# Attention and a GELU block on one core: k of the first batch through SyncE's hardware queue as fp32, masks of the first batch on VectorE, loads and squares in another order

## The chip, the core and the metric

The kernel runs on one core of a Trainium2 chip. The metric is the device time of one launch in microseconds (us), as a median of runs. The core has TensorE (PE in the profile; PEld is its weight load), VectorE (DVE), ScalarE (ACT), GpSimd (POOL) and SyncE (SP). POOL and SP also issue transfers: POOL the ones that change the type on the way, SP the plain ones and the DMA transposes. An engine, and a queue of transfers, works strictly in the order in which its instructions were written: an instruction that waits holds up all behind it.

## The reference

Inputs are q, k, v (8 batches, 8 heads, 576 positions, head size 64), s (8, 8, 576) and two matrices. Cut to what matters:

```python
scores = q @ k.T / 8                                   # per batch and head
cum = cumsum(maximum(s, 0), axis=-1)
bias = -(cum[:, :, :, None] - cum[:, :, None, :])      # decay
scores = where(causal, -1e9, scores + minimum(bias, 0.0))
attn = softmax(scores)
x = (attn @ v).transpose(0, 2, 1, 3).reshape(4608, 512)
g = gelu_exact(x @ w_in)                               # w_in 512 x 2048
out = g @ w_out                                        # w_out 2048 x 512
```

The decay makes far positions vanish, so the kernel computes only a band of blocks: a query block of 128 takes its own key block and the one before. The factor exp(cum) is put on v and on the denominator, so that the exponential of the scores needs no bias. Measures taken on the way (largest |q| and |k|, largest sum of squares of v, the decay) certify at the end that this was allowed; a general path behind a branch, which these inputs don't take, does the rest.

## The kernel before, in words

**Two streams, interleaved by hand.** The GELU block works on chunks of 512 tokens, 9 in all (c = 0 to 8). Chunk c has a layer 1 (`l1_item`, L430: 8 items of 8 matmuls, their results turned into gT by one GELU on ACT each) and a layer 2 (`l2_item`, L450: 4 subtiles of 128 tokens, 16 matmuls each, copied to o_sb and stored by SP). Attention runs one batch ahead: while chunk c is in its layer 2, the attention of batch b = c + 1 is put between its matmuls. The list `side` has 16 places, one behind each quarter (4 matmuls) of a subtile, and holds what is done there: `sc` (scores and their exponentials), `mk` (mask), `av` (product with v, with a division by the denominator on DVE) and `to_xT`.

**One batch of attention.** q and k are loaded as bf16 by POOL (`load_qk`, L85: per tensor and group of four heads four transfers of 147 KB of input each), transposed by DVE (`tr_qk`, L180: one instruction for each of q and k and group g), multiplied (`scores`, L315), turned into P by two exponentials on ACT per unit u, two units per group (`sc_item`, L329), and masked on the diagonal by DVE (`mk_item`, L340: one multiplication for u = 0, two for u = 1). v is loaded as fp32 into raw_v (two buffers, tag rawv), scaled on DVE (`scale_v`, L202) and squared on ACT (`square_v`, L194). The result x of 128 tokens becomes a column block of xT, the input of layer 1, either by a DMA transpose on SP or by TensorE and a copy on DVE (`to_xT`, L383).

**Tokens and batches don't line up.** A batch has 576 tokens, a chunk 512. Chunk 0 needs tokens 0 to 511 of batch 0; chunk 1 needs the last 64 tokens of batch 0 and blocks 0 to 3 of batch 1. In chunk 0's layer 2, blocks 0 and 1 of batch 1 go by DMA transpose on SP, blocks 2 and 3 by TensorE in place 15.

**The first batch** (L486 to L524) has nothing to hide behind. Fillers (`filler`, L397: matmuls of zeros) keep TensorE running. POOL loads q and k of batch 0, then v of batch 0, the four parts of w_in, and so on (L124, L150, L490 to L500). POOL may have eight transfers under way; the ninth waits for the first. `sc_first` (L353) is the first batch's own score function: per pair of heads it does the score matmuls, adds a mask by matmuls of `ident_bf` with `neg_bf` (L374), one filler, and one exponential (L379). Chunk 0's layer 1 is done in two halves of 256 tokens, with the rest of batch 0's attention (list `late`) between the first half's items.

**Behind chunk 0's layer 2** stand on ACT five squares of v, one exponential for the certificate (L242) and the load of the GELU table (L475). In the later chunks the squares stand in layer 1, one behind each of five items, and the table is loaded in layer 2 right behind the last exponentials.

**SP's order around chunk 0's layer 2**: `load_v(2, nc.sync)` is written at the start of subtile 3 (L591), ahead of the `av` in place 12 whose result is block 1 of batch 1.

Of the kernel before, what the change touches and what calls it, by code (L numbers as in the profile page):

```python
# [19 lines left out]
def kernel(  # L20
# [10 lines left out]
    nc = tc.nc  # L31
# [10 lines left out]
    ST = 5  # L42
# [78 lines left out]

    s_sw = const.tile([64, S], fp32, name="s_sw")
    nc.sync.dma_start(out=s_sw, in_=s.flatten_outer_dims())
    load_qk(0, 0, 0)  # L124
    load_qk(0, 1, 0)
# [25 lines left out]
    load_qk(0, 1, 1)  # L151
# [21 lines left out]
    neg_bf = const.tile([128, 128], bf16, name="neg_bf")  # L173

    def masks():
        nc.vector.tensor_scalar(neg_bf, uptri, 30000.0, -30000.0, op0=MULT, op1=ALU.add)
        nc.vector.tensor_copy(ident_bf, ident)
        nc.vector.tensor_copy(tri_bf, uptri)
# [59 lines left out]

    def cert_decay():

        w64 = work.tile([64, S], fp32, tag="w64", bufs=1, name="w64")
        nc.scalar.activation(w64, cum, func=AF.Exp)  # L242
# [110 lines left out]
    def sc_first(g, u):  # L353
# [6 lines left out]
        for h2 in range(2):  # L360
            s_ps = ps.tile([128, 2, 512], fp32, tag="sc", bufs=2, name="sc_ps")
            for jt, i0, n, off in UNITS[u]:
                for e in range(2):
                    for h in range(2):
# [5 lines left out]
                            start=(e == 0), stop=False, tile_position=(h0, 0),  # L370
                        )
                m = min(n, 128)
                for h in range(2):
                    nc.tensor.matmul(  # L374
                        s_ps[:, h, off : off + m], lhsT=ident_bf, rhs=neg_bf[:, :m],
                        start=False, stop=True,
                    )
# [111 lines left out]
    filler(5)  # L489
    load_v(0, nc.gpsimd, range(2))  # L490
    load_w(0, 0)
    load_v(0, nc.gpsimd, range(2, ST))
    for i in range(1, 4):
        load_w(0, i)
    for g in range(HG):
        load_w(1, 2 * g)
        load_w(1, 2 * g + 1)
        for i in range(2):
            load_qk(1, i, g)
    load_v(1, nc.gpsimd)  # L500
    tr_qk(0, 0, 0)
    masks()
    tr_qk(0, 1, 0)
    sc_first(0, 0)
    sc_first(0, 1)
    den_col(0)
    tr_qk(0, 0, 1)
    tr_qk(0, 1, 1)
    filler(4)
    for st in range(2):  # L510
        scale_v(0, st)
    sc_first(1, 0)
    av_item(0, 0, 0)
    av_item(0, 0, 1)
    sc_first(1, 1)
    av_item(0, 1, 0)
    av_item(0, 1, 1)
    filler(2)
# [3 lines left out]
    for st in range(2, ST):  # L522
        scale_v(0, st)
# [8 lines left out]
    for c in range(NCH):  # L532
# [4 lines left out]
        if c == 0:  # L537

            late = [
                [(av, 0, 0, 2)], [(av, 0, 1, 2)], [(av, 0, 0, 3)], [(av, 0, 1, 3), (to_xT, 0, 2, True)],  # L540
                [(av, 0, 0, 4)], [(av, 0, 1, 4), (to_xT, 0, 3, True)], [], [(to_xT, 0, 4, True)],
            ]
            for half in range(2):
                for f2 in range(FT // 2):
# [3 lines left out]
                    if half == 1 and 1 <= f2 <= ST:  # L548
                        square_v(0, f2 - 1)
# [222 lines left out]
```

## Time and profile before

| | |
|---|---|
| median of 9 runs | 337.07 us (335.15 to 339.44) |
| profiled execution | 335.62 us, of which span 333.9 us |
| granted TensorE clock, mean | 0.979 |
| PE busy | 310.4 us, 93% of the span |
| DVE, ACT, POOL busy | 190.3, 185.1, 91.9 us |
| first layer 1 matmul of chunk 0, of chunk 1 | 24.57, 71.13 us |
| first layer 2 matmul of chunk 0, of chunk 1 | 40.77, 86.92 us |

Times of the trace count from the start of the span. A row of the timeline gives the start, the length, engine, line, operation, output and input, how many instructions it holds, and in brackets how long the engine stood before it and what ended that. "DMA" as what ended a wait is a transfer's landing. A row of the windows gives busy time and number of instructions of each engine in a stretch, then the granted clock (PEclk, 1.00 is full), the DMA engines' share and GB/s. SPq and POOLq rows are the issue of transfers.

### The profile page before, as it was taken

What the parts mean: (1) busy time and instruction counts of PE and PEld (TensorE: products, weight loads), DVE (VectorE), ACT (ScalarE), POOL (GpSimd) and SP (SyncE); (2) the same over time, 40 slices, a digit from 0 to 9 for tenths busy, and PEclk for the clock granted to TensorE, in tenths of its full rate; (3) what the DMA queues carried; (4) which work ended last, traced back from release to release, by engine and by line L of the source; (5) the groups of instructions that cost most, each with busy time, mean ns of one, the idle gap of its engine ahead of it and who ended that gap; (6) DMA issues with size and microseconds to landing.
All of it is one profiled execution on the core that took longest, in us unless ns stands there. A gap on an engine that the chain in (4) does not pass through costs nothing.

```text
span 333.9 us, 6297 instructions
## 1 busy us (share of the span) xinstructions
PE 310.4 (93%) x2512; PEld 156.9 (47%) x2554; DVE 190.3 (57%) x393; ACT 185.1 (55%) x247; POOL 91.9 (28%) x152
## 2 busy tenths in 40 slices
PE   8999979649998999899999999999999999999992
PEld 3349824324454544454445454545554545444440
DVE  7356817689446955686459656965695532150020
ACT  2465855638753776377657755874586554205400
POOL 8962759409750037002900380000000000000000
PEclk9999989959999999999999999999999999999997
DMA  8999999999992829381977296602210221110011
GB/s 90 145 232 205 141 162 241 188 241 146 89 157 83 179 25 175 71 189 24 154 136 173 28 174 134 148 8 72 89 31 13 76 81 31 41 63 32 3 66 69
DMA packets 92373, 36.76 MB, mean 110 GB/s; under 512 B 82992, under 2 KB 87088, under 8 KB 92336
## 3 DMA queue, kind: packets, MB, share of 16 engines
q0 software_dynamic: 43872, 16.00, 40.3%
q1 hardware_dynamic: 48464, 20.28, 23.2%
q8 instruction: 22, 0.36, 0.5%
q14 instruction: 15, 0.12, 0.1%
HBM read 36.85 MB, written 9.44 MB: 139 GB/s over the span
## 4 chain that ended last, share of the span: by engine, by line
PE 78%; DMA 10%; POOL 4%; issue 3%; DVE 2%; ACT 1%; POOLq 0%
PE o_ps L457 35%; PE h_ps L441 33%; DMA w_out_r<-in_moe_w_out_dram 7%; PE av L409 5%; PE sc_ps L321 5%; POOL raw_qk L91 3%; DMA w_in_r<-in_moe_w_in_dram 2%; DMA xT<-x 1%; DVE P L344 1%; ACT sq L197 1%; DVE o_sb L467 1%; POOL raw_v L113 1%; DVE x L419 0%; POOL w_out_r L137 0%; ACT w L242 0%
## 5 line engine op out<-in xcount | busy, mean ns | idle before, releaser
L441 PE MATMUL h_ps<-xT,w_in_r 128*128 128x512 bf16 (+1 forms) x624 | 132.8, 360 | 8.5 <-DMA xT<-x 7.1
L457 PE MATMUL o_ps<-w_out_r,gT 128*128 128x512 bf16 x552 | 133.5, 383 | 4.7 <-DMA w_out_r<-in_moe_w_out_dram 2.4
L446 ACT ACTIVATE gT<-h_ps 128x1024 bf16<-128x1024 f32 (+1 forms) x80 | 75.0, 939 | 74.3 <-PE h_ps L441 73.6
L441 PEld LDWEIGHTS <-w_in_r 128*128 128x128 bf16 x640 | 60.0, 98 | 62.1 <-DMA xT<-x 7.3
L457 PEld LDWEIGHTS <-gT 128*128 128x128 bf16 x576 | 52.6, 98 | 60.9 <-issue 7.7
L336 ACT ACTIVATE P<-sc_ps 128x1024 bf16<-128x1024 f32 x56 | 54.3, 1021 | 35.9 <-PE sc_ps L321 35.9
L91 POOL DMA_DIRECT2D raw_qk<-in_q_dram x64 | 38.5, 609 | 91.6 <-DVE amx L189 75.2
L467 DVE COPY o_sb<-o_ps 128x512 f32<-128x512 f32 x32 | 22.1, 692 | 63.8 <-PE o_ps L457 63.8
L91 POOL DMA_DIRECT2D raw_qk<-in_k_dram x64 | 38.4, 607 | 13.0 <-DMA w_out_r<-in_moe_w_out_dram 8.0
L189 DVE TENSOR_REDUCE amx<-raw_qk 128x2 f32<-128x2304 bf16 x16 | 40.2, 2536 | 0.0
L418 DVE RECIPROCAL rc<-av 128x4 f32<-128x4 f32 (+1 forms) x80 | 14.3, 179 | 42.0 <-PE av L409 41.8
L409 PEld LDWEIGHTS <-P 128*128 128x128 bf16 x576 | 27.2, 98 | 18.3 <-DVE P L344 3.1
L419 DVE TENSOR_TENSOR x<-av,rc 128x256 bf16<-128x256 f32 (+1 forms) x80 | 33.8, 423 | 2.8
L409 PE MATMUL av<-vv,P 128*128 128x65 bf16 x576 | 30.7, 193 | 1.9 <-DVE P L344 1.9
L205 DVE TENSOR_TENSOR vv<-raw_v,wb 128x512 bf16<-128x512 f32 (+1 forms) x40 | 25.9, 691 | 2.9 <-DMA raw_v<-in_v_dram 2.9
L182 DVE STREAM_TRANSPOSE qkT<-raw_qk 128x576 f32<-128x576 f32 x32 | 23.2, 758 | 6.6 <-DMA raw_qk<-in_q_dram 3.4
L344 DVE TENSOR_TENSOR P<-P,tri_bf 128x1024 bf16<-128x1024 bf16 x28 | 19.2, 687 | 12.1 <-ACT P L336 11.9
L197 ACT ACTIVATE sq<-raw_v 128x512 bf16<-128x512 f32 (+1 forms) x40 | 24.8, 622 | 0.0
L321 PE MATMUL sc_ps<-qkT 32*128 32x256 bf16 (+2 forms) x560 | 18.0, 250 | 0.0
L321 PEld LDWEIGHTS <-qkT 32*128 32x128 bf16 x560 | 11.6, 92 | 12.6 <-issue 11.9
L401 PE MATMUL f_ps<-zero 128*128 128x512 bf16 x34 | 11.8, 462 | 1.3 <-DVE zero L140 1.2
L379 ACT ACTIVATE P<-sc_ps 128x1024 bf16<-128x1024 f32 x8 | 8.2, 1024 | 6.8 <-PE sc_ps L374 6.8
(74 smaller groups left out, 98.1 us busy)
## 6 DMA issues: line engine op xcount, KB each, us to landing
out_dram<-o_sb SPq DMA_DIRECT2D x36, 256.0 KB, 2.2
raw_v<-in_v_dram SPq DMA_DIRECT2D x24, 256.0 KB, 3.9
raw_qk<-in_q_dram POOLq DMA_DIRECT2D x64, 72.0 KB, 3.3
raw_qk<-in_k_dram POOLq DMA_DIRECT2D x64, 72.0 KB, 3.8
raw_v<-in_v_dram POOLq DMA_DIRECT2D x8, 256.0 KB, 4.8
w_in_r<-in_moe_w_in_dram POOLq DMA_DIRECT2D x4, 512.0 KB, 10.2
w_out_r<-in_moe_w_out_dram POOLq DMA_DIRECT2D x4, 512.0 KB, 11.7
raw_v<-in_v_dram SPq DMA_DIRECT2D x6, 128.0 KB, 3.8
```

What stands on the lines that cost most here:

```text
L91: nc.gpsimd.dma_start(out=raws[b, "qk"][h * 32 : h * 32 + 32, i, g, :].rearrange("p (t c) -> p t c", c=2 * D), in_=bass.AP(tensor=src.tens ...
L189: nc.vector.tensor_reduce(amx[:, b * HG + g], raws[b, "qk"][:, :, g, :], axis=AX, op=ALU.max, apply_absolute_value=True,)
L197: nc.scalar.activation(sq[:n_st], raws[b, "v"][:n_st, st].rearrange("p h d -> p (h d)"), func=AF.Square, accum_out=sumv[:n_st, b, st : st ...
L205: nc.vector.tensor_tensor(vv[b % 2][:n_st, st, :, 0:D], raws[b, "v"][:n_st, st, :, :], w.unsqueeze(2).to_broadcast([n_st, H, D]), op=MULT,)
L321: nc.tensor.matmul(s_ps[h // 2][:, h % 2, off : off + n], lhsT=qk[r, 1, g, jt * 128 : jt * 128 + 128, e], rhs=qk[r, 0, g, i0 : i0 + n, e], ...
L336: nc.scalar.activation(P[:, 2 * h2 : 2 * h2 + 2, o : o + 512], s_ps[h2], func=AF.Exp, scale=scale)
L409: nc.tensor.matmul(o_ps[:, h, :], lhsT=P[:, h, off : off + 128], rhs=vv[b % 2][:, jt, 4 * g + h, :], start=(i == 0), stop=(i == len(BLK[it ...
L419: nc.vector.tensor_tensor(x_of[b, it][:n, g * 256 : g * 256 + 256].rearrange("p (h d) -> p h d", d=D), o_ps[:n, :, 0:D], rc[:n].unsqueeze( ...
L441: nc.tensor.matmul(h_ps[:, i, :], lhsT=w_in_r[:, ko, ft * 128 : (ft + 1) * 128], rhs=xT[:, ko, c * NB + n0 : c * NB + n1], start=(ko == 0) ...
L446: nc.scalar.activation(gT_of[c][:, f2 * 2 : f2 * 2 + 2, n0:n1], h_ps, func=AF.Gelu)
L457: nc.tensor.matmul(y_of[c, sub], lhsT=gT[:, ft, sub * 128 : (sub + 1) * 128], rhs=w_out_r[:, ft, :], start=(ft == 0), stop=(ft == FT - 1),)
L467: nc.vector.tensor_copy(o_sb, y_of[c, sub])
```

## The change

It has these parts.

1. **k of batch 0.** `load_k0` loads it as fp32 into `k0_st` with eight plain transfers on SP (both calls pass `nc.sync`). `cast_k0` turns it into bf16: ACT the first 576 columns of a group, DVE the others. POOL no longer loads it. `k0_st` takes one turn of the two rawv buffers, so raw_v of batch 1 now takes the buffer that held `k0_st`, and raw_v of batch 2 that of batch 0.
2. **POOL's order.** v and w_in of batch 0 alternate more finely, and all four parts of w_out stand ahead of q and k of batch 1.
3. **Masks of batch 0.** The mask matmuls and `neg_bf` go. `mk_item` on DVE masks batch 0 as it does the others: four multiplications for units 0 and 1 of the two groups, and two small ones. Eight fillers instead of five stand behind the weights; four go, one comes in front of `to_xT`, and three are put between the two transposes in place 15 of chunk 0.
4. **Chunk 0, layer 1.** Blocks 3 and 4 of v are scaled between the items; squares of v of batch 0 stand behind items 3, 5 and 7 of the first half, the last two at the start of layer 2.
5. **Chunk 0, layer 2.** The places in `side` shift by about one. `load_v(2, nc.sync)` comes behind all four subtiles and `load_qks(2)`.
6. **Squares and certificate.** Batch 1's squares go into chunk 1's layer 1. From chunk 1 on the squares of the next batch leave layer 1 and stand in layer 2, between the last exponentials and the load of the GELU table. `cert_decay`'s exponential goes to place 3 of chunk 1's layer 2, its small DVE operations behind chunk 2's layer 1.

```diff
+    k0_st = work.tile([128, HG, S * 2], fp32, tag="rawv", bufs=2, name="k0_st")
+    def load_k0(g, eng):
+        for h in range(4):
+            eng.dma_start(
+                out=k0_st[h * 32 : h * 32 + 32, g, :].rearrange("p (t c) -> p t c", c=2 * D),
+                in_=bass.AP(tensor=k.tensor, offset=k.offset + (4 * g + h) * S * D,
+                            ap=[[2 * D, 32], [64 * D, SB], [1, 2 * D]]),
+            )
+    def cast_k0(g):
+        nc.scalar.activation(raws[0, "qk"][:, 1, g, :S], k0_st[:, g, :S], func=AF.Copy)
+        nc.vector.tensor_copy(raws[0, "qk"][:, 1, g, S:], k0_st[:, g, S:])
...
+    load_k0(0, nc.sync)
+    load_k0(1, nc.sync)
     load_qk(0, 0, 0)
-    load_qk(0, 1, 0)
...
-                            start=(e == 0), stop=False, tile_position=(h0, 0),
+                            start=(e == 0), stop=(e == 1), tile_position=(h0, 0),
                         )
-                m = min(n, 128)
-                for h in range(2):
-                    nc.tensor.matmul(
-                        s_ps[:, h, off : off + m], lhsT=ident_bf, rhs=neg_bf[:, :m],
-                        start=False, stop=True,
-                    )
...
     tr_qk(0, 0, 0)
+    cast_k0(0)
+    tr_qk(0, 1, 0)
     masks()
...
     sc_first(0, 1)
+    mk_item(0, 0, 0)
+    sc_first(1, 0)
...
     sc_first(1, 1)
+    filler(2)
+    mk_item(0, 1, 0)
...
     to_xT(0, 1, True)
-    for st in range(2, ST):
-        scale_v(0, st)
+    mk_item(0, 0, 1)
+    scale_v(0, 2)
+    mk_item(0, 1, 1)
     gelu_set()
...
-                side[15] = [(to_xT, b, 2, True), (to_xT, b, 3, True)]
+                side[15] = [(to_xT, b, 2, True), (filler, 3), (to_xT, b, 3, True)]
                 for sub in range(4):
-                    if sub == 3:
-                        load_v(2, nc.sync)
                     groups(c, (sub,), side[4 * sub : 4 * sub + 4])
...
                 load_qks(2)
+                load_v(2, nc.sync)
...
                     side[at].append((sc, b, g, u))
+                for st in range(ST):
+                    side[sc_at[3]].append((square_v, b, st))
                 side[sc_at[3]].append((gelu_set,))
```

On POOL, between the loads of q and k of batch 0 and those of batch 1, the order before is this (raw_qk holds q and k, raw_v holds v, w_in_r and w_out_r the matrices):

```order
L91 DMA raw_qk<-in_q_dram 32x9x128 x4
L91 DMA raw_qk<-in_k_dram 32x9x128 x4
L113 DMA raw_v<-in_v_dram 128x8x64 x2
L137 DMA w_in_r<-in_moe_w_in_dram 128x4x512
L113 DMA raw_v<-in_v_dram 128x8x64 x2
L113 DMA raw_v<-in_v_dram 64x8x64
L137 DMA w_in_r<-in_moe_w_in_dram 128x4x512 x3
L137 DMA w_out_r<-in_moe_w_out_dram 128x4x512 x2
L91 DMA raw_qk<-in_q_dram 32x9x128 x4
L91 DMA raw_qk<-in_k_dram 32x9x128 x4
L137 DMA w_out_r<-in_moe_w_out_dram 128x4x512 x2
```

The same place of POOL's queue in the changed kernel, from the second load of q of batch 0 on:

```order
L91 DMA raw_qk<-in_q_dram 32x9x128 x4
L113 DMA raw_v<-in_v_dram 128x8x64 x2
L156 DMA w_in_r<-in_moe_w_in_dram 128x4x512
L113 DMA raw_v<-in_v_dram 128x8x64
L156 DMA w_in_r<-in_moe_w_in_dram 128x4x512
L113 DMA raw_v<-in_v_dram 128x8x64
L113 DMA raw_v<-in_v_dram 64x8x64
L156 DMA w_in_r<-in_moe_w_in_dram 128x4x512 x2
L156 DMA w_out_r<-in_moe_w_out_dram 128x4x512 x4
L91 DMA raw_qk<-in_q_dram 32x9x128 x4
L91 DMA raw_qk<-in_k_dram 32x9x128 x4
```

The loads of k of batch 0 are gone from ahead of v, and the last two parts of w_out have moved ahead of the eight loads of q and k.

SP's queue from the start to chunk 1 before (out_dram<-o_sb is the store of a subtile, xT<-x the DMA transpose of a block of x; the raw_v rows are first batch 2, then batch 3):

```order
L123 DMA s_sw<-in_s_dram 64x576
L469 DMA out_dram<-o_sb 128x512 x3
L388 DMA_TRANSPOSE xT<-x 128x4x128
L113 DMA raw_v<-in_v_dram 128x8x64 x4
L113 DMA raw_v<-in_v_dram 64x8x64
L388 DMA_TRANSPOSE xT<-x 128x4x128
L469 DMA out_dram<-o_sb 128x512
```

The same in the changed kernel:

```order
L141 DMA s_sw<-in_s_dram 64x576
L127 DMA k_st<-in_k_dram 32x9x128 x8
L480 DMA out_dram<-o_sb 128x512 x3
L399 DMA_TRANSPOSE xT<-x 128x4x128 x2
L480 DMA out_dram<-o_sb 128x512
L113 DMA raw_v<-in_v_dram 128x8x64 x4
L113 DMA raw_v<-in_v_dram 64x8x64
```

Eight loads of k stand behind s, and both transposes of x now stand ahead of v of batch 2.

On DVE, where the first batch gives way to chunk 0's layer 1, the order before is this (xT<-xt_ps is the copy of a block of xT, vv<-raw_v,wb is `scale_v`, rc and x belong to an `av`):

```order
L395 COPY xT<-xt_ps 128x4x128 x2
L205 TENSOR_TENSOR vv_102<-raw_v,wb 128x8x64 x2
L205 TENSOR_TENSOR vv_102<-raw_v,wb 64x8x64
L418 RECIPROCAL rc<-av 128x4
L419 TENSOR_TENSOR x<-av,rc 128x256
```

In the changed kernel (P<-P,tri_bf is `mk_item`):

```order
L406 COPY xT<-xt_ps 128x4x128 x2
L361 TENSOR_TENSOR P<-P,tri_bf 128x4x2x128
L366 TENSOR_TENSOR P<-P,tri_bf 128x4x64
L220 TENSOR_TENSOR vv_103<-raw_v,wb 128x8x64
L361 TENSOR_TENSOR P<-P,tri_bf 128x4x2x128
L366 TENSOR_TENSOR P<-P,tri_bf 128x4x64
L429 RECIPROCAL rc<-av 128x4
L430 TENSOR_TENSOR x<-av,rc 128x256
```

Both masks of unit 1 have come in ahead of the first `av` of the layer, and one scaling instead of three stands there; the other two now stand between later `av`s.

More of the change, by code (lines that the diff above doesn't have):

```diff
@@ L237, in le, with cert_exp @@
         nc.vector.tensor_scalar(dst, a, float(thr), None, op0=op)
+    w64 = work.tile([64, S], fp32, tag="w64", bufs=1, name="w64")
+    def cert_exp():
+        nc.scalar.activation(w64, cum, func=AF.Exp)
     def cert_decay():
[L241 to L242 removed]
         W = const.tile([64, ST], fp32, name="cW")
```

78 lines of the change are left out of this document (42 added, 36 removed).

## Prediction

> **What bounds the kernel now.** I first read the cores view: span 333.9 us at a mean granted clock of 0.979. The page gives PE 93% of the span, so what can be won is where PE stands, or runs below full clock. The view of waits, whole span, names two waits of PE over 2 us, both for transfers:
>
> ```profile
> PE h_ps L441 <- DMA xT<-x: 7.1, 1, 7.1
> PE o_ps L457 <- DMA w_out_r<-in_moe_w_out_dram: 2.4, 2, 2.1
> ```
>
> The timeline of PE puts them at the two borders of chunk 0's layer 2:
>
> ```profile
> 24.57 1.03 PE L441 MATMUL h_ps<-xT,w_in_r 128*128 128x256 bf16 x8 [0.52 <-DVE xT L395]
> ...
> 40.77 1.89 PE L457 MATMUL o_ps<-w_out_r,gT 128*128 128x512 bf16 x7
> 42.94 1.02 PE L457 MATMUL o_ps<-w_out_r,gT 128*128 128x512 bf16 x4 [0.28 <-DMA w_out_r<-in_moe_w_out_dram]
> ...
> 46.63 4.44 PE L457 MATMUL o_ps<-w_out_r,gT 128*128 128x512 bf16 x12 [2.11 <-DMA w_out_r<-in_moe_w_out_dram]
> ...
> 63.27 0.74 PE L392 MATMUL xt_ps<-ident_bf,x 128*128 128x128 bf16 x8
> 71.13 3.39 PE L441 MATMUL h_ps<-xT,w_in_r 128*128 128x512 bf16 x8 [7.12 <-DMA xT<-x]
> ```
>
> Layer 1 starts at 24.57, layer 2 at 40.77, chunk 1 at 71.13. Behind each wait the matmuls are slow, and the windows say why:
>
> ```profile
> 24.57:33.77 9.20, 9.20 (x125) 8.22 (x124) 5.92 (x17) 4.30 (x8) 1.81 (x3) 1.00 1.25 204
> ...
> 40.77:46.63 5.86, 3.42 (x29) 1.49 (x28) 0.10 (x1) 4.72 (x7) 2.02 (x4) 1.00 1.24 165
> 46.63:51.00 4.37, 4.37 (x12) 1.47 (x12) 2.15 (x3) 0.60 (x1) 4.12 (x5) 0.61 1.25 176
> ...
> 63.30:71.10 7.80, 0.71 (x9) 0.41 (x7) 4.22 (x17) 5.51 (x13) 0.00 (x0) 0.76 1.24 229
> ```
>
> After a stretch with PE busy 3.42 of 5.86 us, the granted clock is 0.61 (column behind POOL), and 12 matmuls take 4.37 us. What they take at full clock is in the chain of work that ended last, in layer 1 of chunk 1:
>
> ```profile
> 76.73 7.34 PE h_ps L441 x34
> ```
>
> That is 0.216 us each (0.86 for a quarter, 1.73 for eight), so 12 take 2.59. The w_out waits cost 0.28 + 2.11 + (4.37 - 2.59) = 4.2 us. The x wait costs 7.12 us and, with eight matmuls in 3.39 instead of 1.73, another 1.66. The last column but one shows the DMA engines full all the while (1.24 to 1.25; it sums overlapping packets).
>
> **Why x comes late.** SP's queue, timeline:
>
> ```profile
> 60.43 1.31 SPq L388 DMA_TRANSPOSE xT<-x  x1
> 61.93 6.03 SPq L113 DMA_DIRECT2D raw_v<-in_v_dram  x5
> 68.07 1.24 SPq L388 DMA_TRANSPOSE xT<-x  x1
> ```
>
> Block 1's transpose stands behind five loads of v that take 6.03 us to issue, and lands 3.0 us later (68.07 to 71.08). The change puts both transposes ahead of v. What is late next: TensorE's own blocks 2 and 3 with two copies, and the transpose, if it is slow:
>
> ```profile
> DMA to landing us min/median/max: 3.0/3.6/5.3
> ```
>
> **POOL's queue**, from its timeline:
>
> ```profile
> 3.82 2.46 POOL L91 DMA_DIRECT2D raw_qk<-in_k_dram  x4
> ...
> 9.30 2.38 POOL L91 DMA_DIRECT2D raw_qk<-in_k_dram  x4
> 11.68 1.81 POOL L113 DMA_DIRECT2D raw_v<-in_v_dram  x2
> ...
> 33.87 0.60 POOL L91 DMA_DIRECT2D raw_qk<-in_k_dram  x1 [1.98 <-DMA w_out_r<-in_moe_w_out_dram]
> 36.38 0.60 POOL L91 DMA_DIRECT2D raw_qk<-in_k_dram  x1 [1.91 <-DMA w_out_r<-in_moe_w_out_dram]
> ...
> 43.18 0.60 POOL L91 DMA_DIRECT2D raw_qk<-in_k_dram  x1 [1.00 <-DMA w_out_r<-in_moe_w_out_dram]
> 46.88 0.60 POOL L91 DMA_DIRECT2D raw_qk<-in_k_dram  x1 [3.09 <-DMA w_out_r<-in_moe_w_out_dram]
> 47.47 0.91 POOL L113 DMA_DIRECT2D raw_v<-in_v_dram  x1
> ```
>
> The bracketed waits date the landings: the four parts of w_out at 33.9, 36.4, 43.2 and 46.9, so 2.5 us a part alone, up to 3.7 beside others. Without k's two sets (2.46 + 2.38) all behind comes 4.8 us sooner: 29.1 and 31.6; the last two follow directly, at 2.5 to 3.7 each 36.6 to 39.0.
>
> **The first batch, new.** ACT's cast of k stands behind its weights, and DVE's transpose behind the cast:
>
> ```profile
> 7.90 0.20 ACT L229 ACTIVATE wb<-t_ps 64x64 bf16<-64x64 f32 x1
> 9.31 0.40 PE L366 MATMUL sc_ps<-qkT 32*128 32x256 bf16 x4 [0.54 <-DVE qkT L182]
> 10.52 1.02 ACT L379 ACTIVATE P<-sc_ps 128x1024 bf16<-128x1024 f32 x1 [2.41 <-PE sc_ps L374]
> 11.84 1.02 ACT L379 ACTIVATE P<-sc_ps 128x1024 bf16<-128x1024 f32 x1 [0.29 <-PE sc_ps L374]
> ...
> 22.07 1.02 ACT L379 ACTIVATE P<-sc_ps 128x1024 bf16<-128x1024 f32 x1 [0.56 <-PE sc_ps L374]
> ```
>
> The durations come from the groups:
>
> ```profile
> L182 DVE STREAM_TRANSPOSE qkT<-raw_qk 128x576 f32<-128x576 f32 x32 | 23.2, 758 | 6.6 <-DMA raw_qk<-in_q_dram 3.4 <-DMA raw_qk<-in_k_dram 3.2
> L242 ACT ACTIVATE w<-cum 64x576 f32<-64x576 f32 x1 | 0.7, 671 | 0.0
> L344 DVE TENSOR_TENSOR P<-P,tri_bf 128x1024 bf16<-128x1024 bf16 x28 | 19.2, 687 | 12.1 <-ACT P L336 11.9
> L349 DVE TENSOR_TENSOR P<-P,tri_bf 128x256 bf16<-128x256 bf16 x14 | 4.0, 285 | 0.0
> L205 DVE TENSOR_TENSOR vv<-raw_v,wb 128x512 bf16<-128x512 f32 x32 | 21.1, 693 | 2.9 <-DMA raw_v<-in_v_dram 2.9
> L197 ACT ACTIVATE sq<-raw_v 128x512 bf16<-128x512 f32 x32 | 19.9, 623 | 0.0
> ```
>
> No row shows the cast itself; the nearest is L242, 576 columns on ACT, 0.67 us. First scores: 8.10 + 0.67 + 0.76 and a little = 9.65, 0.34 later than 9.31. From there ACT sets the pace, not PE: a part's score matmuls were followed by mask matmuls, and exponentials stood 1.3 apart or more. Without the masks eight exponentials of 1.02 with one cast of 0.67 between and some 0.2 of gaps follow 10.45 and end at 19.5; they ended at 23.09. VectorE's masks of unit 0 (0.69 each) lie beside that. With the same tail (products, division, two PE transposes, copies), partly beside the last exponential, layer 1 starts at about 21.5 instead of 24.57: 3.1 us won. w_in's first part lands by then, being 4.8 us sooner like all of POOL's queue.
>
> **Layer 1 of chunk 0 gives some back.** DVE was busy 5.92 of the first half's 9.20 us; the masks of unit 1 add 2 x (0.687 + 0.285) = 1.94, and they come late. After the copies of xT (21.45) DVE does mask, scaling, mask, so block 2's first product waits for 21.45 + 0.97 + 0.69 = 23.1, and PE is there after its first item (eight half matmuls, 0.87), at 22.4: 0.75 lost. The scalings of blocks 3 and 4, each between two divisions and a third, come about 0.55 and 0.85 behind PE in the same way. Sum 2.15, bounds 0 and 3 (all of 1.94 plus the late scalings on the path). Layer 2 then starts at 40.77 - 3.1 + 2.15 = 39.8: **1.0 us** won.
>
> **Layer 2 of chunk 0.** w_out is complete at 36.6 to 39.0, needed from 39.8 on, its last part at 42.4: the **4.2 us** go. q and k of batch 1's first group now come behind w_out. Before, the eight and w_out's third part landed between 36.4 and 43.2; less 2.5 to 3.7 for the part, eight take 3.1 to 4.3 us. So they land at 39.7 to 43.3, and two transposes end at 41.2 to 44.8; their scores stand in place 3, at 39.8 + 4 x 0.86 = 43.2. I take 0, bounds 0 to 1.6. v of batch 1 is issued 4 us sooner than 47.47 and where its first part was scaled 3.7 later; it is needed at place 7, about 47.8 us: covered by a fraction of 1 us, and by 2 more until its product in place 9. If k of batch 0 didn't ride for free (below), these two covers are what goes.
>
> **Border to chunk 1.** Layer 2 ran from 40.77 to 64.0; without 4.2 and with three fillers (0.65) it takes 19.7, and ends at 59.5. x of block 1 comes from place 12, three quarters (2.6) and some products and fillers ahead of that, so at about 55.5; its transpose, behind block 0's 1.3 us of issue, goes out by 55.8 and lands at 58.8 (3.0) or 61.1 (5.3). The two copies on DVE end about 0.6 behind PE. So chunk 1 starts at 60.1, bounds 59.7 and 61.5, at full clock: against 71.13 + 1.66 = 72.8 that is 12.7 us, of which 1.0 and 4.2 are counted above and **7.5** are this border's. v of batch 2, now issued from 60 to 66, is wanted by DVE behind 5 us of maxima and four transposes at 68, so it is covered or costs DVE 2 us, which PE doesn't feel before its layer 2.
>
> **The later chunks.** Five squares move between the last exponentials and the table, seen at chunk 3's end:
>
> ```profile
> 203.56 1.28 ACT L475 ACT_TABLE_LOAD   x1
> 206.95 1.02 ACT L446 ACTIVATE gT<-h_ps 128x1024 bf16<-128x1024 f32 x1 [2.10 <-PE h_ps L441]
> 208.85 1.03 ACT L446 ACTIVATE gT<-h_ps 128x1024 bf16<-128x1024 f32 x1 [0.88 <-PE h_ps L441]
> ```
>
> Five take 3.07 us back to back (0.623 each, overlapped). The table is then there at 203.56 + 3.07 + 1.28 = 207.9, the first GELU 0.95 late, its buffer free at 208.9; PE begins the third item when the second one's results are there, at 208.85. I put 0.1 us on each of four such borders (chunks 3 to 6; in 1 and 2 the last exponentials are one place earlier): 0.4 lost, bounds 0 and 2. In layer 1 the squares' absence wins nothing, since PE was not waiting there.
>
> **Sum.** 1.0 + 4.2 + 7.5 - 0.4 = 12.3; I take off 0.3 for small waits: 12.0. The profiled execution, 335.62 us, becomes 323.6. It lay 1.45 us under the median of the runs, 337.07, so the median becomes **325.0**.
>
> **Two rules weighed.** The clock: a window with PE 58% busy, its longest wait 2.11 us, was followed by 0.61; the one from 24.57, fully busy, stayed at 1.00. The Trainium skill, "TensorE: Matmul & The Clock Gate", Part 1, has the clock fall after an idle window of about 3.4 us; by that alone the wait of 2.11 would have cost no clock, the w_out term would be 2.4 instead of 4.2, and the result 326.8; this trace contradicts it, with 12 matmuls in 4.37 us. The same page, under "A second HAM failure mode", has the clock also fall through frequent small idles between groups of matmuls, which speaks against this change and would give the time of rival C. The transfers: k's eight cost POOL 4.84 us of issue. The Trainium skill, "DMA: Bandwidth & Descriptors", section "Issuing engines are not separate DMA queues", says that a second issuing engine saves only the issue time, since all run on the same 16 DMA engines; that gives the sum above where the engines have room, and the time of rival B where they have none.
>
> **Rivals.** B: k's fp32 still takes the DMA engines' time. Eight loads take 3.1 to 4.3 us of them (above), so only some 1.1 of the 4.8 us are won, w_out ends at 40.3 to 42.7 and batch 1's first group is transposed at 45 to 48, 3 us after place 3; then v is late as well, and k of batch 0 may hold ACT's second cast by up to 2. Against it: before, POOL's issue of 0.6 us each set the first 12 us, above the 0.4 to 0.5 that the engines need. The 3 us and 1 more make 329. C: the first batch's PE, now waiting for ACT, and layer 1 with its three stalls fall to the slow clock; 4 to 6 us at 0.61 cost about 2.5: 327.5. Against it: even with stalls PE is busy 9.2 of 11.35 us, 81%. D, slower than before: the squares hold up the GELU table at all four later borders by more than the two h_ps buffers bear. That decides from 1 us of further delay on; with all of 3.07 + 1.28 exposed, 4 x 4.35 = 17.4 us are lost against 12.3 won: 342. Against it: the sum above ends within 0.1 us of the point, and each item behind it lets ACT catch up by 1.73 - 1.02 = 0.7. E: the change doesn't do what it says: the idle stretch at the border comes back because block 1's x itself is late, not its place in SP's queue, so that only the 1.0 and part of the 4.2 us go: 335. Against it: the transpose went out 0.11 us behind the last load of v (67.96, 68.07), so the queue set it.
>
> **Numbers.** Forecast 0.55 (own range 322 to 328), B 0.2, C 0.12, D 0.04, E 0.02; 0.07 for more than forecast (no stall in layer 1, no loss later: 321). Low 321, high 330.5, which takes in B and C. A difference of 0.5% (1.7 us) is about what a measurement of this kernel can tell from no change. Faster: all but D and E's half and some of B's tail, 0.93; same 0.03; slower 0.04.
>
> **What would show it.** Right: layer 1 near 21.5 with short waits for DVE before three products; no wait for w_out and clock 1.00 from 40 on; chunk 1 near 60 with PE idle under 1.5 us; later chunks of the same length within 0.2 us. Wrong: a wait of PE for raw_qk, raw_v or xT over 2 us in chunk 0, a window there below clock 0.9, or first GELUs that PE waits for.

## The result, and the profile after

The changed kernel takes 327.87 us (median of 10 runs, 326.06 to 330.08) against 337.07 (31 runs, 335.12 to 339.44): a ratio of 0.9729, interval 0.9698 to 0.9759. The forecast was 325.0, its range 321 to 330.5. The time lies 2.9 us above the forecast and 0.4 from rival C's 327.5. The profiled execution took 328.70 us and has a span of 326.9 us instead of 333.9, at a mean granted clock of 0.977. So the medians give 9.2 us and the two profiled executions 6.9: the first lay 1.45 us under its median, the second lies 0.83 above.

The view of waits of the changed kernel, PE alone (wait; us in total, times, longest): both waits for transfers over 2 us are gone, and one for q and k of the first batch is new.

```profile
PE sc_ps L383 <- DVE qkT L197: 1.7, 1, 1.7
PE av L420 <- DVE vv L220: 1.3, 3, 0.5
...
PE h_ps L452 <- DVE xT L406: 1.0, 2, 0.5
```

PE's timeline after gives the stages: the first scores, layer 1 of chunk 0 with its three stalls, layer 2, chunk 1.

```profile
10.58 0.63 PE L383 MATMUL sc_ps<-qkT 32*128 32x256 bf16 x8 [1.70 <-DVE qkT L197]
...
26.59 1.03 PE L452 MATMUL h_ps<-xT,w_in_r 128*128 128x256 bf16 x8 [0.51 <-DVE xT L406]
28.00 0.37 PE L420 MATMUL av<-vv,P 128*128 128x65 bf16 x7 [0.34 <-DVE vv L220]
30.82 0.37 PE L420 MATMUL av<-vv,P 128*128 128x65 bf16 x7 [0.43 <-DVE vv L220]
33.96 0.37 PE L420 MATMUL av<-vv,P 128*128 128x65 bf16 x7 [0.53 <-DVE vv L220]
...
44.57 2.75 PE L468 MATMUL o_ps<-w_out_r,gT 128*128 128x512 bf16 x11
...
65.34 1.89 PE L452 MATMUL h_ps<-xT,w_in_r 128*128 128x512 bf16 x8 [0.52 <-DVE xT L406]
```

The windows of the same stages after (behind POOL: granted clock, DMA share, GB/s):

```profile
12.31:25.20 12.89, 12.67 (x101) 6.59 (x101) 6.78 (x15) 8.94 (x9) 7.61 (x12) 0.50 1.17 217
26.59:44.57 17.98, 16.67 (x189) 14.70 (x188) 14.30 (x27) 10.78 (x21) 9.17 (x15) 1.00 1.30 168
44.57:64.82 20.25, 19.64 (x209) 10.31 (x211) 11.94 (x30) 13.51 (x19) 12.47 (x20) 1.00 1.00 171
```

Before, the first of these stretches ran at full clock:

```profile
12.31:25.20 12.89, 12.04 (x143) 6.13 (x144) 6.19 (x16) 7.98 (x8) 9.96 (x14) 1.00 1.10 210
```

So layer 1 of chunk 0 starts 2.0 us later than before instead of 3.1 sooner, and takes 17.98 us instead of 16.20. From layer 2's start to chunk 1's it takes 20.77 instead of 30.36, and chunk 1's first eight matmuls take 1.89 instead of 3.39. The balance of the spans: 2.0 + 1.8 - 9.6 - 1.5 + 0.3 (later chunks) = -7.0.

Why the first scores are late stands on DVE. After:

```profile
8.52 0.78 DVE L197 STREAM_TRANSPOSE qkT<-raw_qk 128x576 f32<-128x576 f32 x1 [2.26 <-DMA raw_qk<-in_q_dram]
9.22 0.42 DVE L138 CAST raw_qk<-k_st 128x576 bf16<-128x576 f32 x1
9.74 0.78 DVE L197 STREAM_TRANSPOSE qkT<-raw_qk 128x576 f32<-128x576 f32 x1
```

Before, q was there when DVE came to it:

```profile
6.48 0.76 DVE L182 STREAM_TRANSPOSE qkT<-raw_qk 128x576 f32<-128x576 f32 x1
```

What is late is q. ACT's cast of k starts at 8.04, where the forecast had 8.10; behind q's transpose, DVE's half of the cast (9.22 to 9.64) then stands ahead of k's. The loads of q take 4.6 us from issue to landing in the first 12 us (median, DMA issues after), where before it was 2.6:

```profile
k_st<-in_k_dram SPq DMA_DIRECT2D x8, 144.0 KB, 5.2
...
raw_qk<-in_q_dram POOLq DMA_DIRECT2D x8, 72.0 KB, 4.6
```

**Two theories.** Theory 1: k's fp32 transfers share the DMA engines with q's, so q is some 2 us late, PE waits 1.70 us, and the clock falls to 0.5. Theory 2: the clock falls because the first batch, now paced by ACT, leaves PE many small gaps; q has nothing to do with it.

### The profile page after: what moved, and what is told of

The parts are those of the page before. It is cut to its first block, busy times and chain, and to the rows that moved or that the text cites. A ratio compares the mean times of both kernels' runs of the same rounds, so it can differ in the third digit from the quotient of the medians.

```text
span 326.9 us, 6258 instructions
## 1 busy us (share of the span) xinstructions
PE 309.8 (95%) x2478; PEld 158.6 (49%) x2519; DVE 193.3 (59%) x400; ACT 186.7 (57%) x249; POOL 88.5 (27%) x144
## 3 DMA queue, kind: packets, MB, share of 16 engines
q0 software_dynamic: 41440, 15.41, 39.0%
## 4 chain that ended last, share of the span: by engine, by line
PE 88%; DVE 6%; issue 2%; DMA 2%; POOL 0%; DVEq 0%; POOLq 0%
PE h_ps L452 37%; PE o_ps L468 36%; PE av L420 6%; PE sc_ps L338 5%; PE sc_ps L383 2%; PE f_ps L412 2%; DMA raw_qk<-in_q_dram 2%; DVE P L361 1%; DVE x L430 1%; DVE vv L220 1%; DVE o_sb L478 1%; DVE xT L406 0%; PE xt_ps L403 0%; DVE rc L429 0%; POOL raw_qk L91 0%
## 5 line engine op out<-in xcount | busy, mean ns | idle before, releaser
L468 PE MATMUL o_ps<-w_out_r,gT 128*128 128x512 bf16 x551 | 131.6, 379 | 2.5 <-issue 1.7
L468 PEld LDWEIGHTS <-gT 128*128 128x128 bf16 x576 | 52.0, 98 | 57.3 <-issue 3.0
L420 PEld LDWEIGHTS <-P 128*128 128x128 bf16 x576 | 28.1, 99 | 20.7 <-DVE P L361 3.5
L91 POOL DMA_DIRECT2D raw_qk<-in_k_dram x56 | 33.6, 609 | 8.6 <-DMA w_out_r<-in_moe_w_out_dram 7.8
L420 PE MATMUL av<-vv,P 128*128 128x65 bf16 x576 | 32.0, 195 | 3.6 <-DVE P L361 1.9
L361 DVE TENSOR_TENSOR P<-P,tri_bf 128x1024 bf16<-128x1024 bf16 x32 | 21.9, 685 | 12.4 <-ACT P L353 12.4
L412 PE MATMUL f_ps<-zero 128*128 128x512 bf16 x40 | 15.0, 498 | 1.2 <-DVE zero L159 1.2
```

The lines of the kernel that those rows point to most:

```text
L91: nc.gpsimd.dma_start(out=raws[b, "qk"][h * 32 : h * 32 + 32, i, g, :].rearrange("p (t c) -> p t c", c=2 * D), in_=bass.AP(tensor=src.tens ...
L361: nc.vector.tensor_tensor(d, d, tri_bf.unsqueeze(1).unsqueeze(1).to_broadcast([128, 4, 2, 128]), op=MULT)
L420: nc.tensor.matmul(o_ps[:, h, :], lhsT=P[:, h, off : off + 128], rhs=vv[b % 2][:, jt, 4 * g + h, :], start=(i == 0), stop=(i == len(BLK[it ...
L468: nc.tensor.matmul(y_of[c, sub], lhsT=gT[:, ft, sub * 128 : (sub + 1) * 128], rhs=w_out_r[:, ft, :], start=(ft == 0), stop=(ft == FT - 1),)
```

## The experiments

**Eight more fillers behind the weights.** They cover the wait and leave q as late as it is.

```diff
     weights()
-    filler(8)
+    filler(16)
```

> The changed kernel with 16 instead of 8 fillers behind the weights, so that TensorE works on zeros while it waits for k of batch 0 (it stood 1.70 us there). Theory 1: that wait let the clock fall to 0.5 from 11.5 to 25 us. Then the clock stays at 1.00 in 11 to 25 us, layer 1 of chunk 0 starts near 22.5 instead of 26.6, and the kernel takes some 3 to 4 us less than the changed one, about 324. Theory 2 (rival): the clock fell because the first batch's matmuls now come in small groups with pauses for ScalarE. Then it falls all the same, a little later, and the time stays within 1 us of the changed kernel's 327.9.

328.10 us (6 runs, ratio 0.9707, 0.9661 to 0.9754): not theory 1's 324, though the first batch does what theory 1 says. PE's timeline of this run:

```profile
22.17 1.03 PE L452 MATMUL h_ps<-xT,w_in_r 128*128 128x256 bf16 x8 [0.52 <-DVE xT L406]
...
63.67 2.97 PE L452 MATMUL h_ps<-xT,w_in_r 128*128 128x512 bf16 x8 [3.28 <-DMA xT<-x]
```

Its windows:

```profile
12.31:25.20 12.89, 11.45 (x151) 7.70 (x149) 10.26 (x25) 9.97 (x12) 7.38 (x11) 1.00 1.12 206
...
63.67:66.64 2.97, 2.97 (x12) 1.24 (x13) 2.10 (x1) 0.00 (x0) 0.57 (x1) 0.61 1.25 282
```

PE is less busy in the first batch than in the changed kernel (11.45 us of 12.89 instead of 12.67), the gaps of theory 2 are all there, and the clock is 1.00: theory 2 falls. Layer 1 starts 4.4 us sooner. Chunk 1, which now waits for SP's DMA transposes of x, starts only 1.7 us sooner and then runs slowly; its layer 2 starts at 79.64, where the changed kernel has 79.63, so all of the 4.4 us is gone. The transposes go out 4.4 us sooner (55.93 instead of 60.36), among batch 2's q and k, whose loads POOL issues until 58.6. The DMA issues of the stretch from 40 to 72 us, in this run:

```profile
xT<-x SPq DMA_TRANSPOSE x2, 6.1
```

In the changed kernel, from 44 to 76 us:

```profile
xT<-x SPq DMA_TRANSPOSE x2, 2.4
```

So the border is bound by the DMA engines as soon as the first batch is right.

**k of batch 0 by POOL as bf16 again**, without the cast:

```diff
-    load_k0(0, nc.sync)
-    load_k0(1, nc.sync)
     load_qk(0, 0, 0)
+    load_qk(0, 1, 0)
...
     load_qk(0, 0, 1)
+    load_qk(0, 1, 1)
...
-    cast_k0(0)
-    cast_k0(1)
```

> The changed kernel with one part undone: k of batch 0 is again loaded as bf16 by POOL in its old places, with no fp32 tile and no cast. Theory 1 (k's transfers on SP share the DMA engines with q's, so that both came 2 us later, and the wait dropped the clock): q's first group is transposed at 6.5 instead of 8.5, first scores at 9.3 instead of 10.6, the clock stays at 1.00, layer 1 starts at 21.5 to 22.5; POOL's queue is 4.8 us later, so w_out ends at 41 to 43 and costs up to 1 us; in sum 2 to 4 us less than the changed kernel. Rival: the move of k is what makes the change gain at the start, and without it w_out and batch 1 come too late: 2 to 4 us more than the changed kernel.

331.62 us (4 runs, 0.9809, 0.9751 to 0.9867): slower, as the rival had it. But DVE transposes q at 6.48 as before, so the lateness of q was k's doing, and theory 1's first link holds:

```profile
6.48 0.76 DVE L196 STREAM_TRANSPOSE qkT<-raw_qk 128x576 f32<-128x576 f32 x1
```

However, k of group 1 is now late, and POOL's whole queue behind it. PE's timeline (lines are one less here):

```profile
14.65 0.63 PE L382 MATMUL sc_ps<-qkT 32*128 32x256 bf16 x8 [1.68 <-DVE qkT L196]
...
66.85 3.07 PE L451 MATMUL h_ps<-xT,w_in_r 128*128 128x512 bf16 x8 [3.32 <-DMA xT<-x]
```

The clock falls to 0.52 behind the wait of 1.68, and x is late again. Loading k by SP is worth 3.7 us by the medians (331.62 less 327.87) and 2.7 by the ratios, in spite of what it does to q.

**v of batch 2 at the start of subtile 3 again:**

```diff
                 for sub in range(4):
+                    if sub == 3:
+                        load_v(2, nc.sync)
                     groups(c, (sub,), side[4 * sub : 4 * sub + 4])
                 gelu_set()
                 load_qks(2)
-                load_v(2, nc.sync)
```

> The changed kernel with v of batch 2 loaded at the start of subtile 3 again, ahead of the second transpose of x. If the place in SP's queue is what made the 7 us wait at the border to chunk 1, the wait comes back with its slow clock: 6 to 8 us more than the changed kernel. If x's block 1 would have been in time anyway, since all comes earlier or v's buffer is free earlier, less than 2 us.

335.03 us (4 runs, 0.9893, 0.983 to 0.9957): 7.2 us lost by the medians, 5.5 by the ratios, about as expected. SP's timeline shows block 1's transpose behind v:

```profile
61.71 1.33 SPq L399 DMA_TRANSPOSE xT<-x  x1
63.27 4.03 SPq L113 DMA_DIRECT2D raw_v<-in_v_dram  x5
67.39 1.25 SPq L399 DMA_TRANSPOSE xT<-x  x1
```

PE waits 4.27 us for it, and chunk 1 starts at 70.44 with eight matmuls in 3.50 us. The first scores also waited longer in this run (2.70), so its layer 1 starts 1.35 us later. From the start of layer 2 to the end of chunk 1's first eight matmuls it takes 28.03 us instead of 22.66: the border itself costs 5.4.

**The first late mask and scaling ahead of a product** (`mk_item(0, 0, 1)` and `scale_v(0, 2)` moved in front of `av_item(0, 1, 0)`):

> The changed kernel with the mask of unit 1 of group 0 and the scaling of block 2 done ahead of the products of group 1, where VectorE stands idle, instead of behind the copies of xT. If the three waits for VectorE in the first half of layer 1 (0.5 us each and what hangs on them, 1.8 us in all) come from VectorE's order, the first one goes and the second and third shrink: 0.5 to 1.5 us less than the changed kernel. If VectorE is simply full there, no change.

328.93 us (4 runs, 0.9744, 0.9687 to 0.9801). The first stall of layer 1 is gone (1.0 us in two waits instead of 1.3 in three), but the first scores waited 2.32 in this run, and chunk 1 starts at 65.38, as in the changed kernel (65.34). Nothing can be told by the time.

**The last two parts of w_out behind batch 1's first q and k again:**

```diff
-    for i in range(4):
-        load_w(1, i)
-    load_qks(1)
+    load_w(1, 0)
+    load_w(1, 1)
+    for i in range(2):
+        load_qk(1, i, 0)
+    load_w(1, 2)
+    load_w(1, 3)
+    for i in range(2):
+        load_qk(1, i, 1)
```

> The changed kernel with the last two parts of w_out back behind batch 1's q and k of group 0, as the kernel before had them. Theory of the prediction's step on w_out (its waits cost 4.2 us with their slow clock): layer 2 of chunk 0 waits again for parts 2 and 3, 3 to 4.5 us, 331 to 332.5. Rival (the later layer 2, 44.57 for 40.77, hides two thirds of the waits already): a wait under 1 us, 327.5 to 329.

329.18 us (4 runs, 0.9763, 0.9733 to 0.9793). No wait for w_out comes back, as the rival had it, and by the ratios the two kernels can't be told apart. POOL's timeline dates the landing of the last two parts (the ends of its waits):

```profile
40.48 0.61 POOL L91 DMA_DIRECT2D raw_qk<-in_k_dram  x1 [1.87 <-DMA w_out_r<-in_moe_w_out_dram]
44.02 0.60 POOL L91 DMA_DIRECT2D raw_qk<-in_k_dram  x1 [2.93 <-DMA w_out_r<-in_moe_w_out_dram]
```

Before, they landed at 43.18 and 46.88, and layer 2 started at 40.77; here it starts at 42.94 and wants the last part 2.6 us on, at 45.5. So k's move off POOL brings the last part 2.9 us sooner and layer 2 comes 2.2 later, and together that is enough; the new order only adds to it. With layer 2 at the forecast's 39.8, the last part, wanted at 42.4, would be 1.6 us late (an estimate from these rows). What does come back is a wait for x at the border of 1.45 us.

**v of batch 2 behind the x tiles, alone, in the kernel before:**

```diff
                 for sub in range(4):
-                    if sub == 3:
-                        load_v(2, nc.sync)
...
                 load_qks(2)
+                load_v(2, nc.sync)
```

> The kernel before with one part of the change alone: v of batch 2 is issued behind the x tiles' transposes instead of ahead of subtile 3. Theory: this part alone is the border's 7.5 to 9 us (chunk 1 starts at 62 to 64 instead of 71.13 and without its slow clock of 1.66): 328 to 330.5 us, so that the rest of the change gives nothing net. Rival (the border's gain needs the w_out weights and the q and k of batch 1 earlier as well): 333 or more, with a wait on a DMA at the border left.

332.11 us (4 runs, 0.9864, 0.9815 to 0.9912): between the theories in time, and the rival's in kind. PE's timeline:

```profile
47.53 2.75 PE L457 MATMUL o_ps<-w_out_r,gT 128*128 128x512 bf16 x12 [2.14 <-DMA w_out_r<-in_moe_w_out_dram]
...
68.89 1.89 PE L441 MATMUL h_ps<-xT,w_in_r 128*128 128x512 bf16 x8 [3.10 <-DMA xT<-x]
```

The w_out waits stay, and 3.10 of the 7.12 us for x: the transposes, issued from 62.24 on, take 5.1 and 5.2 us to land, in DMA engines that are full (a share of 1.34 to 1.87 from 62 to 68 us). This part gives 5.0 us alone by the medians (337.07 less 332.11) and 4.6 by the ratio. Not all of that is its own: the twelve matmuls behind the wait for w_out take 2.75 us here and took 4.44, and the part doesn't reach them.

**Blocks 0 and 1 of batch 1 by TensorE**, with the eight fillers:

```diff
-                side[11] = [(av, b, 0, 2), (av, b, 1, 0), (scale_v, b, 4)]
-                side[12] = [(av, b, 1, 1), (av, b, 0, 3)]
-                side[13] = [(mk, b, 1, 1)]
+                side[11] = [(av, b, 0, 2), (av, b, 1, 0, True), (scale_v, b, 4)]
+                side[12] = [(av, b, 1, 1, True), (av, b, 0, 3), (to_xT, b, 0, True)]
+                side[13] = [(mk, b, 1, 1), (to_xT, b, 1, True)]
```

> Eight fillers more behind the weights, as in the run with them alone, and batch 1's x blocks 0 and 1 go into xT by TensorE transposes instead of two DMA transposes. Theory (the border after the cover is bound by the DMA engines: batch 2's q and k are still landing when the two DMA transposes are issued at 55.9, so they land 6.1 us later and layer 1 of chunk 1 waits 3.28): the wait on the DMA goes, chunk 1 starts at 61.0 to 61.8 instead of 63.67 with 2.97 of slow clock, its layer 2 4 us sooner than 79.80, and the time is 4 us below the 328.1 of the cover alone: 323.5 to 325. Rival (something else, DVE at 3.4 to 3.6 of 4 us there or the loads of the next batch, sets the border as well): chunk 1's layer 2 starts within 1 us of 79.80 again, 327 to 328.5.

324.84 us (5 runs, 324.36 to 325.91; ratio 0.963, 0.9605 to 0.9656), each at a clock of 0.994 or more. PE's timeline:

```profile
22.44 1.03 PE L452 MATMUL h_ps<-xT,w_in_r 128*128 128x256 bf16 x8 [0.52 <-DVE xT L406]
...
56.93 0.40 PE L403 MATMUL xt_ps<-ident_bf,x 128*128 128x128 bf16 x4 [0.72 <-DVE x L430]
...
62.24 1.89 PE L452 MATMUL h_ps<-xT,w_in_r 128*128 128x512 bf16 x8 [0.52 <-DVE xT L406]
```

The wait on the DMA is gone, and both gains stay. This is the fastest of the kernels tried, 1.0% below the changed one by the ratios (0.963 against 0.9729, their intervals apart).

**The same without the fillers:**

> Only batch 1's x blocks 0 and 1 by TensorE transposes, without the eight fillers. Theory: in the changed kernel the border's DMA transposes have landed when they are wanted (no wait on a DMA there), so nothing is gained, and 8 transposes lie on TensorE, 0.39 us for four: 0 to +1 us, 327.5 to 329. Rival (the border's transposes cost something there too): 326 or less.

Two kinds of runs, which neither theory had: 324.70 and 324.80 us at a clock of 0.997 and 0.996, the other five at 328.98 to 332.58 and 0.972 to 0.979 (median of the seven 330.37). PE's timeline of the longest, which was profiled:

```profile
12.13 1.03 PE L383 MATMUL sc_ps<-qkT 32*128 32x256 bf16 x8 [3.00 <-DVE qkT L197]
...
29.50 1.03 PE L452 MATMUL h_ps<-xT,w_in_r 128*128 128x256 bf16 x8 [0.52 <-DVE xT L406]
```

The clock from 12 to 28 us is 0.51. With x off the DMA, the later start costs its full price: layer 1 comes 7.06 us later than with the fillers (29.50 for 22.44), and so does chunk 1 (69.30 for 62.24). The run at 328.98 lies 4.2 us above the two at the high clock, of which neither has a trace. In the changed kernel the border hides most of such a difference: two of its runs had a clock of 0.995 and 0.994, and took 326.06 and 326.35 us, 1.5 to 1.8 below the median.

**Half of k: group 0 by SP as fp32, group 1 by POOL as bf16.**

```diff
-    load_k0(1, nc.sync)
...
     load_qk(0, 0, 1)
+    load_qk(0, 1, 1)
...
-    cast_k0(1)
```

> The changed kernel with k of batch 0's group 1 back on POOL as bf16 (no cast of it), group 0 still by SP as fp32: half as many fp32 transfers beside q. Theory 1 (q and k share the DMA engines): q of group 0 lands 1 us sooner, 7.2 to 7.6 instead of 8.4, the first scores wait 0.3 to 1.0 instead of 1.70, the clock stays at 1.00, layer 1 starts at 22.5 to 24. Since POOL has four loads more ahead of the rest, the loads of the next batches end 2.4 us later and x waits for its DMA transposes at the border as with the cover: 327 to 329 us. Rival (q is late because of POOL's own order, the fp32 transfers do not matter): q of group 0 still at 8.2 to 8.5, the wait still 1.5 or more and the clock at 0.5.

329.01 us (6 runs, 0.978, 0.9732 to 0.9828). q is transposed at 7.53 instead of 8.52, and the first scores wait 0.17: theory 1. But POOL's four further loads delay v of batch 0 now, and PE's timeline shows the next wait:

```profile
16.54 0.54 PE L420 MATMUL av<-vv,P 128*128 128x65 bf16 x7 [0.99 <-DVE vv L220]
...
65.30 1.89 PE L452 MATMUL h_ps<-xT,w_in_r 128*128 128x512 bf16 x8 [2.90 <-DMA xT<-x]
```

From 16 to 20 us the clock is 0.52. The expectation that it stays at 1.00 failed; the wait for x came as expected. The clock isn't all that counts here: the two runs with the highest mean, 0.986 and 0.989, are the slowest (331.44 and 330.81).

**Half of k with the TensorE transposes:**

> The run before it plus batch 1's x blocks 0 and 1 by TensorE transposes. Theory: with a full clock in the first batch and no DMA at the border, chunk 1 starts at 61.5 to 62.5, 323.8 to 325.5 us, without the eight fillers. Rival (group 1's k by POOL comes too late and the clock falls in the first batch after all): layer 1 at 26 or later, 328 to 331, or runs of both kinds as with the TensorE transposes alone.

328.15 us (6 runs, 0.974, 0.9693 to 0.9787), the rival's time. With the same start, q is transposed at 8.20 here, the first scores wait 0.95, and the clock from 12 to 20 us is 0.53. But a run at a mean clock of 0.996 took 327.71 us, only 0.4 below the median, so the slow clock isn't what holds this kernel back most; what does stays open, since that run has no trace.

**The same with the eight fillers:**

> Both edits of the run before it and the eight fillers. Theory: like the fillers with the TensorE transposes (324.84), within 0.7: 324.0 to 325.5, every run at a clock of 0.99 or more. Rival (the DMA engines' load of batches 1 and 2, 2.4 us later by POOL's four loads more, reaches TensorE through the scores of batch 1): 326 or more with a wait of scores or of scaled v on a DMA.

326.08 us (7 runs, 0.967, 0.963 to 0.9711), the rival's case, slower than 324.84 with all of k by SP. In the profiled execution, the slowest (328.55), a product waits 1.48 us for scaled v at 17.47, and the clock from 16 to 24 us is 0.63. The other six lie at 325.92 to 326.62 with a clock of 0.994 or more, so the microsecond beside 324.84 isn't the clock's.

**Squares of batches 3 to 7 back in layer 1**, on top of the fillers with the TensorE transposes:

```diff
                 if c == 1 and 1 <= f2 <= ST:
                     square_v(c, f2 - 1)
+                if c > 1 and b < B and 1 <= f2 <= ST:
+                    square_v(b, f2 - 1)
...
-                for st in range(ST):
+                for st in range(ST if c == 1 else 0):
                     side[sc_at[3]].append((square_v, b, st))
```

> The fillers with the TensorE transposes, and the squares of v of batches 3 to 7 back in layer 1 of the chunk before, as the kernel before had them. The prediction's step on the squares (0.1 us lost on each of four borders because the GELU table's load comes behind five squares): chunks 2 to 5 shorter by 0.1 each, 324.4 beside 324.84, which these rounds can hardly tell by the time; the borders in the trace do, 32.4 instead of 32.5 from chunk 4's start to chunk 5's. Rival (squares in layer 1 hold up the GELUs that layer 1's PSUM buffers wait for): those chunks longer, 325.5 or more.

324.96 us (6 runs, 0.9637, 0.9597 to 0.9677): the same by the time. PE's timeline has the starts of chunks 5 and 6:

```profile
194.31 1.89 PE L452 MATMUL h_ps<-xT,w_in_r 128*128 128x512 bf16 x8
...
226.82 1.89 PE L452 MATMUL h_ps<-xT,w_in_r 128*128 128x512 bf16 x8
```

With the squares in layer 2 (the fillers with the TensorE transposes):

```profile
195.03 1.89 PE L452 MATMUL h_ps<-xT,w_in_r 128*128 128x512 bf16 x8
...
227.62 1.89 PE L452 MATMUL h_ps<-xT,w_in_r 128*128 128x512 bf16 x8
```

32.51 us instead of 32.59: the squares in layer 2 cost 0.08 there. Chunk 3 takes 32.02 instead of 32.48, where the next chunk's first item had waited 0.28 for a square; the changed kernel, whose chunk 3 takes 32.03, has no such wait.

**All first batches side by side**, each from its profile: PE's longest wait between 9 and 18 us, the lowest clock of the windows of 4 us from 12 to 28 us, and the starts of chunk 0's layer 1 and of chunk 1.

| kernel | wait, at | clock | layer 1 | chunk 1 |
|---|---|---|---|---|
| eight fillers | 0.53, 15.41 | 1.00 | 22.17 | 63.67 |
| fillers, TensorE transposes | 0.53, 15.68 | 1.00 | 22.44 | 62.24 |
| the last, squares in layer 1 | 0.53, 15.39 | 1.00 | 22.15 | 61.98 |
| the kernel before | 0.54, 9.31 | 1.00 | 24.57 | 71.13 |
| before with v moved | 0.70, 9.22 | 1.00 | 24.47 | 68.89 |
| half of k, TensorE transposes | 0.95, 10.26 | 0.50 | 24.72 | 64.51 |
| half of k | 0.99, 16.54 | 0.52 | 24.18 | 65.30 |
| w_out late | 1.03, 10.48 | 0.50 | 24.96 | 64.63 |
| half of k, fillers, transposes | 1.48, 17.47 | 0.50 | 25.15 | 65.27 |
| k by POOL | 1.68, 14.65 | 0.52 | 24.71 | 66.85 |
| changed kernel | 1.70, 10.58 | 0.50 | 26.59 | 65.34 |
| mask early | 2.32, 11.23 | 0.50 | 27.14 | 65.38 |
| v early | 2.70, 12.02 | 0.50 | 27.94 | 70.44 |
| TensorE transposes alone | 3.00, 12.13 | 0.50 | 29.50 | 69.30 |

In this stage every profile with a wait of 0.95 us or more has the slow clock behind it, and none with 0.70 or less.

## Why the prediction was right or wrong

**First batch, 3.1 us won: wrong**, the step that failed. "First scores: 8.10 + 0.67 + 0.76 and a little = 9.65" priced the cast (0.67; it took 0.68) and took q to be there as before. It was transposed 2.0 us later (8.52 for 6.48), and DVE's half of the cast, which the sum leaves out, stood behind it (0.42), so scores start at 10.58; that k's transfers make q late is shown by k on POOL (6.48 again). "From there ACT sets the pace" then failed through the clock: 16.0 us from the first scores to layer 1, where the prediction had 11.85. With the wait covered it is 10.9 (11.27 to 22.17), so ACT's pace itself was sized a little too long. Layer 1 starts at 26.59 instead of the forecast's 21.5; the 5.1 us between are about what the profiled executions lack (6.9 us won, 12.0 forecast).

**Stalls of layer 1, 2.15: right.** The layer takes 1.78 longer (17.98 less 16.20), and 1.30 of that are the waits of the three products named.

**w_out, 4.2: right in size.** The parts are there at 30.18, 32.72, 35.26 and 37.81, within the predicted 29.1 to 39.0. The cause was drawn too narrowly: the old order alone brings no wait back once k is off POOL's queue and layer 2 starts as late as it does.

**Border, 7.5: right in this kernel, by luck.** From layer 2's start it took 20.77 us to chunk 1, predicted 60.1 - 39.8 = 20.3. The prediction let the transposes land in 3.0 to 5.3 us; they took 2.4, because layer 2 came 4.8 us later than forecast and the DMA engines had worked off their queue (POOL's last load of batch 2 is issued by 57.3, the transposes from 60.36). With layer 2 at 40.14, near the forecast's 39.8, they took 6.1, outside the bounds, and the time was 328.10. So 325.0 doesn't come out with the first batch at full clock either (the lowest of the six runs is 326.67): the gain of the first batch and the gain at the border exclude each other as long as x goes by DMA.

**Squares, 0.4: right.** Chunks 4 to 7 grow by 0.08 or 0.09 us each, 0.35 in sum; chunk 3 doesn't. (The rows that the prediction shows for chunk 3's end are those of chunk 4's: chunk 5 starts at 204.96 in that trace.)

**The rivals.** C named the slow clock of the first batch, at 2.5 us, and its time, 327.5, is met by luck. Its causes, the wait for ACT and the three stalls, left the clock at 1.00; behind q's lateness the slow clock and the wait cost 4.4 at layer 1's start, and the border takes most of that back. What it costs in the end is perhaps the 1.8 by which the changed kernel's best run lies below its median; no trace of that run shows it. B named k's transfers in the DMA engines, and put their price at w_out and batch 1; it fell on q of the first batch instead. The Trainium skill, "DMA: Bandwidth & Descriptors", section "Issuing engines are not separate DMA queues", says that transfers of all issuing engines run on the same 16 DMA engines. That is borne out: k on a second queue took q's loads from 2.6 to 4.6 us. D and E fell: 0.1 us a border, and PE waits 0.52 us at chunk 1.

**The rule on the clock.** The Trainium skill, "TensorE: Matmul & The Clock Gate", Part 1, has the clock fall after an idle window of about 3.4 us, which the prediction took for the length of one wait. That reading does not hold: in the first batch 0.95 was enough, and at the border to chunk 1 waits of 3.28 and 3.10 us came out differently. As the length of the steps in which the clock changes it agrees with the traces (3.41 us, last section). The Trainium skill, same page, under "A second HAM failure mode", has frequent small idles between groups of matmuls bring the clock down too. No run here shows it: the gaps alone, with PE busy 11.45 of 12.89 us, kept 1.00.

## What to carry to other kernels

A transfer moved to another queue saves its issue time and still takes its share of the DMA engines: look at what is in flight beside it, above all at a first load that everything waits for. A gain upstream is worth only what the next shared resource lets through; check where its transfers will land if the stage starts as early as you forecast. And where a wait brings the slow clock behind it, as in this first batch, fillers that reach to the first real matmul can be worth more than the wait itself (4.4 us at layer 1's start for a wait of 1.70).

## What the runs showed of the hardware

**The length of one wait doesn't decide the clock.** In the first batch 0.95 us was enough. At the border to chunk 1, waits of 1.45, 2.90 and 3.10 us left the clock at 1.00, and 3.28, 3.32 and 4.27 were followed by eight matmuls in 2.97, 3.07 and 3.50 us instead of 1.89. In layer 2 of chunk 0, a wait of 2.11 was followed by 0.61 before, and one of 2.14, with v moved alone, was not, as the windows of that kernel show (PE busy 2.06 of 5.00 us, clock 1.00):

```profile
43.00:48.00 5.00, 2.06 (x23) 0.93 (x23) 0.60 (x1) 2.61 (x3) 0.83 (x2) 1.00 1.37 169
```

**The clock changes in steps of 3.41 us.** Windows of 0.25 us date each change of the clock. Through the start of chunk 1, all changes of one trace lie whole multiples of 3.41 us apart. In the changed kernel the clock falls at 11.64 and is back at 25.30, four steps later; with k by POOL it changes at 16.19, 23.02, 67.39 and 70.81, which is 2, 15 and 16 steps behind the first. Ahead of each fall stands a step in which PE was less busy than in any step of the same stage behind which the clock stayed:

| stage | clock fell behind steps with PE busy | stayed at 1.00 from |
|---|---|---|
| first batch (from 8 us on) | 12 to 72% (nine traces) | 75% |
| layer 2 of chunk 0 | 38% (the kernel before) | 47% (v moved alone) |
| border to chunk 1 | 2, 4, 16 and 19% | 40% (v moved alone) |

So a wait counts by how much of it falls into one step. The 3.10 us with v moved alone were split over two steps, busy 69 and 40%; the 3.28 us with the eight fillers left 19% in one. The steps don't begin with the kernel: with the TensorE transposes alone, whose first batch is the same code as in the changed kernel, the clock fell at 12.16 instead of 11.64. That this, with q landing at different times behind the same start (transposed at 7.53 and at 8.20), makes the two kinds of runs is argued, not shown: of those two kernels no run at the high clock has a trace.

**What stays open.** The share isn't the whole rule: at 66 to 69% layer 2 kept its clock (v moved alone), and at 70 to 72% the first batch lost it. Nor do the shares say when the clock comes back: in the changed kernel three steps with PE busy throughout didn't bring it, and the fourth, at 93%, did. Why q lands at different times behind the same start is open too.
